# Second layers of stages 5 and 6 by block products, and a shorter conversion of the f64 weights

## The chip, the cores and the metric

One core of one Trainium2 chip. The metric is the device time of the kernel in microseconds (us). TensorE (PE) multiplies, VectorE (DVE), ScalarE (ACT) and GpSimd (POOL) do the elementwise work, SyncE (SP) issues most DMAs. PEld is the loading of a matmul's stationary operand, which runs beside the matmuls. Each engine works through its own queue in order.

## The reference

```python
def reference(q, k, v, probs, w1, w2, w_in, w_out, alpha):
    x = attn(q, k, v)                  # 2 x 8 heads, 576 tokens, head size 64, causal window of 64
    x = x.transpose(0, 2, 1, 3).reshape(1152, 512)
    p = probs / (probs.sum(-1, keepdims=True) + 1e-9)
    y = 0
    for e in range(4):                 # w1[e]: 512 x 1024, w2[e]: 1024 x 512
        y += p[:, e:e+1] * (np.maximum(x @ w1[e], 0) @ w2[e])
    h = y @ w_in                       # 512 x 2048, float64 in memory
    g = np.maximum(h, 0) + alpha * np.minimum(h, 0)
    return (g @ w_out).astype(np.float32)   # w_out: 2048 x 512, float64 in memory
```

## The kernel before

Every matmul operand is split into a high part in fp32r and a low part (the difference), and a product is three matmuls: high x low, low x high, high x high. The high part is made by ACT, the low part by DVE (`low`, L222) or POOL.

After the attention the work goes in stages 0 to 11 of 512 hidden columns each. Stages 0 to 7 are the four experts of the first layer pair (two stages each), stages 8 to 11 the second pair. In each stage from 1 on, the tokens come in two parts: the first 512 (p = 0) and the last 640 (p = 1). The first layer of a part is seven products ("A", 0 to 6) of a Strassen-Winograd scheme over halves of the inner dimension, hidden columns and tokens (`product`, L452). Their sums are built in three PSUM banks X, Z and W that go on accumulating after a partial sum has been copied or added out. An eviction (`evict`, L506) applies the ReLU or the leaky ReLU; for stages 8 and up that is ACT `r`, DVE product with alpha, ACT `hh`, POOL `hl` (`activate`, L553). The second layer of a part is one unit ("B", `l2_unit` L584) per 128 tokens: twelve matmuls of 512 columns into one bank, added by DVE into `acc` (L692, L696). Only the last stage has its second layer of the last 512 tokens in seven block products ("M", `block_product` L646), two groups of six matmuls with 256 columns each, again with banks X, Z and W.

A PSUM bank for a new tile is handed out in the order in which the eight banks fell free.

The order of the units is written out (L787 to 816). Beside each unit, after its matmuls are issued, a planner (`plan`) hangs work on it: the weight sums and splits of the next stage, the splits of this stage's second-layer weights, the sums and splits of x. Low parts of splits are put off to the next unit (`settle`). Loads of weights (`load_w`) are hung on the unit in which the second last tile before them has had its last use.

`w_in` and `w_out` come as float64 words. 32 pieces of 128 x 512 are converted to fp32 and stored to DRAM (`conv_steps`, L264), from where stages 8 to 11 load them. A piece is three steps: two ACT operations on the low and the high word; two DVE operations (clamp, shift) and the store of the piece before; a DVE operation that puts the sign in, and a load two pieces ahead. After these come, at the start of the next step, a DVE operation for the exponent and two POOL operations. How many steps run after a unit is said by `pace` (L917): stages 2 to 6 have 13 a stage, one after every second-layer unit and four in the first layers. `EARLY` = 26 pieces are done by the end of stage 7's first layer, the rest begins in stage 8's second layer of the last 640 tokens.

Of the kernel before, what the change touches and what calls it, by code (L numbers as in the profile page):

```python
# [26 lines left out]
def tile_kernel(ctx, tc, q, k, v, probs, w1, w2, w_in, w_out, alpha, out):  # L27
# [137 lines left out]
    def load_d(n):  # L165
        which, s, f = F64[n]
        o = (s - S1) * FS + f * P
        src = w_in.bitcast(U32)[:, 2 * o:2 * o + 2 * P] if which == 1 else w_out.bitcast(U32)[o:o + P, :]
        t = late["mid"].tile([P, 1024], U32, tag="wd", bufs=2, name=f"wd{n}")
# [89 lines left out]
        while converted[0] < n:  # L259
            next(late["steps"], None)  # L260

    EARLY = 13 * len(F64) // 16

    def conv_steps(first, last):  # L264
        done = []

        def store():
            if done:
                o, y = done.pop(0)
                nc.sync.dma_start(out=o, in_=y)  # L270
                converted[0] += 1

        late["ct"] = big_as("ct").rearrange("p (o m) -> p o m", o=7)
        load_d(first)
        load_d(first + 1)
        yield
        for n, (which, s, f) in list(enumerate(F64))[first:last]:
            ct = late["ct"]
            t = wd_t.pop(n)
            if which == 1:  # L280
                words = t.rearrange("p (k m w) -> p k m w", k=KD, w=2)
                top, low = words[:, :, :, 1], words[:, :, :, 0]
# [163 lines left out]
    tr = {}  # L446
# [52 lines left out]
    def h_tiles(s, p, f):  # L499
        if (s, p, f) not in h_t:  # L500
            pool = late["mid"] if p else sb
            h_t[s, p, f] = [pool.tile([P, LEN[p]], F32R, tag=f"h{w}{p}", bufs=NF, name=f"h{w}{s}_{p}_{f}")
                            for w in "hl"]
        return h_t[s, p, f]

    def evict(s, p, f, half, src, direct=False):  # L506
        c = slice(half * HALF[p], (half + 1) * HALF[p])
        hh, hl = [x[:, c] for x in h_tiles(s, p, f)]
        if s >= S1:
# [43 lines left out]
    def activate(keep, later):  # L553
        while len(heads) > keep:
            hh, hl, r, col, src, g = heads.pop(0)
            nc.vector.scalar_tensor_tensor(out=g, in0=r, scalar=col, in1=src, op0=ALU.mult, op1=ALU.add)
            tails.append((hh, hl, g))
# [151 lines left out]
    with tc.manual_schedule():  # L709
# [68 lines left out]
        def Bt(s, p):  # L778
            return [("B", s, p, t) for t in range(NTT[p])]

        def LC(c):
            return [("LC", c, f) for f in range(NF)]

# [22 lines left out]
                last_use[op] = len(order) - 1  # L806
        order += [("END",)] + LC(3) + [("X1",)] + BC(3)
        for s in range(1, S1):
            order += A(s, 0) + A(s, 1) + Bt(s, 0) + Bt(s, 1)
        order += A(S1, 0) + [("B", S1, 0, t) for t in (2, 3, 0, 1)]  # L810
        order += A(S1, 1) + [("B", S1, 1, t) for t in (3, 4, 0, 1, 2)]
        for s in range(S1 + 1, NST - 1):
            order += A(s, 0) + A(s, 1) + Bt(s, 0) + Bt(s, 1)
# [11 lines left out]
        for s in range(1, NST):  # L825
            if s == 1:
                lc, b = [[(k, NCH - 1, t) for t in range(3)] for k in ("LC", "BC")]
                for u in range(2):
                    plan(lc[u], w_sums, (1, s), s, u, nc.gpsimd)
                for u, part, unit in ((0, A11, ("X1",)), (1, A11, b[0]), (0, SA1, b[0]), (1, SA1, b[1]),  # L830
                                      (0, A22, b[2]), (1, A22, b[2])):
                    plan(unit, w_split, (1, s), s, u, part)
            else:
                b = [("B", s - 1, x, t) for x in range(2) for t in range(NTT[x])]
                if s == S1 + 1:
                    b = [("B", S1, 1, t) for t in (3, 3, 4, 4, 0, 1)]
                late_sums = s > S1 + 1
                behind = 2 * (s > S1 + 1)
                plan(b[1] if behind else ("A", s - 1, 1, 0 if s > S1 else 2), w_sums, (1, s), s, 0, nc.gpsimd)
                for n, part in ((0, A11), (0, A22), (1 + behind, SA1)):  # L840
                    plan(b[n], w_split, (1, s), s, 0, part)
                plan(b[2 + behind], w_sums, (1, s), s, 1, nc.gpsimd)
                for n, part in ((2, A11), (3, A22), (4 + behind, SA1)):
                    plan(b[n], w_split, (1, s), s, 1, part)
            units = [(0, 0), (0, 1), (1, 0), (1, 1)]
            if s in (1, S1):
                units = [(int(s == 1), i) for i in (0, 0, 1, 1)]
            for f, (p, i) in enumerate(units):
# [33 lines left out]
        for unit, splits, sums, e in ((lc[0], (0, 5), (), None), (lc[1], (0,), (), None), (lc[2], (), (1,), nc.vector),  # L882
# [11 lines left out]
        for unit, span in ((("A", 1, 0, 5), (0, EARLY)), (("A", S1, 1, 2), (EARLY, len(F64)))):  # L894
            plan(unit, lambda *a: late.update(steps=conv_steps(*a)) or next(late["steps"]), None, *span)
        plan(("B", S1 - 1, 0, 0), raw_tile, None)
        uses = {}
        for n in sorted(work):
# [17 lines left out]
            load_w(tid)  # L916
        def pace(op, s=0, p=0, i=0):  # L917
            if op == "A":
                return int(2 <= s < S1 and i < 2 or S1 < s < NST - 1 and i < 2)
            if op != "B" or s in (S1 - 1, NST - 2, NST - 1) or (s, p) == (S1, 0) or s > S1 and (p, i) == (0, 0):  # L920
                return 0
            return 1 + (s == 1 and p == 0 and i % 2)

        pend = []
        for i, unit in enumerate(order):
# [9 lines left out]
            if op == "A":  # L935
                product(unit[1], unit[2], 0, unit[3])
                product(unit[1], unit[2], 1, unit[3])
                if unit[3] == 6:
                    low_parts(0)
                    activate(0, 0 if unit[1] == S1 else 4)  # L940
            elif op == "M":
                activate(0, max(0, len(tails) - 1))
                block_product(*unit[1:])
# [17 lines left out]
                fn(*args)  # L961
            for _ in range(pace(*unit)):
                next(late["steps"], None)
            if i == at["A", S1 - 1, 1, 6]:
                convert(EARLY)
# [50 lines left out]
```

## Time and profile before

| | us |
|---|---|
| three runs, median (lowest, highest) | 612.62 (612.18, 613.17) |
| profiled execution | 612.78 |
| its span, first to last instruction | 611.0 |
| PE busy in it | 604.4 |
| DVE busy | 484.1 |
| ACT busy | 321.0 |
| POOL busy | 278.4 |

The profiled execution is one of its own; its time exceeds its span by what lies around the first and the last instruction. Busy times are sums over the whole span; which engine is late in a stage is read from the windows, the waits and the timeline.

### The profile page before, as it was taken

To read this page: it belongs to the slowest core of one execution; us is meant where nothing else is said; L and a number is where in the kernel's file an instruction comes from. 1 tells how busy PE (TensorE), PEld (TensorE's weight loads), DVE (VectorE), ACT (ScalarE), POOL (GpSimd) and SP (SyncE) were. 2 spreads that over 40 slices of the span, in tenths; PEclk is the share of its full clock that TensorE was granted. 3 is DMA by queue.
4 is the path that set the end of the run, shared out by engine and by line. 5 is a ranking of instruction groups with operands and counts; after the bars stand their busy time and mean duration, and the time that the engine had idled before them with its cause. 6 is when DMAs were issued, how large, how long until landed. Compare 5 with 4: busy or idle time off the path is not lost.

```text
span 611.0 us, 11073 instructions
## 1 busy us (share of the span) xinstructions
PE 604.4 (99%) x4108; PEld 549.2 (90%) x4108; DVE 484.1 (79%) x971; ACT 321.0 (53%) x801; POOL 278.4 (46%) x285
## 2 busy tenths in 40 slices
PE   7999999999999999999999999999999999999997
PEld 6898899889889889989989989989898988988987
DVE  4788597799798798798698698657968979756785
ACT  6966356436427426426515625536777653653750
POOL 4815812075153254265152452522755586664450
PEclk9999999999999999999999999999999999999999
DMA  8924005235235225324325323012302402300012
GB/s 277 378 92 139 2 1 162 78 106 165 95 104 156 92 98 170 108 72 170 104 93 152 120 87 104 17 70 78 130 1 74 165 38 82 122 41 1 2 53 103
DMA packets 31830, 62.61 MB, mean 102 GB/s; under 512 B 2464, under 2 KB 11936, under 8 KB 30752
## 3 DMA queue, kind: packets, MB, share of 16 engines
q1 hardware_dynamic: 31056, 61.25, 29.9%
q8 instruction: 32, 0.52, 0.4%
q10 hardware_dynamic: 720, 0.66, 0.3%
q14 instruction: 22, 0.18, 0.1%
HBM read 51.14 MB, written 10.75 MB: 101 GB/s over the span
## 4 chain that ended last, share of the span: by engine, by line
PE 97%; ACT 2%; DMA 1%; DVE 0%; ACTq 0%; issue 0%
PE o L580 42%; PE X L465 23%; PE Z L465 12%; PE W L465 6%; PE h L535 4%; PE oc L568 4%; PE pv L391 1%; ACT p L358 1%; PE pt L374 1%; PE mX L667 1%; PE s L336 1%; DMA kt<-in_k_dram 1%; PE x L706 1%; PE mZ L667 0%; PE mW L667 0%; ACT ptr L380 0%
## 5 line engine op out<-in xcount | busy, mean ns | idle before, releaser
L580 PE MATMUL o<-w2h,hl 128*128 128x512 f32 x380 | 148.2, 390 | 0.0
L580 PE MATMUL o<-w2l,hh 128*128 128x512 f32 x380 | 148.2, 390 | 0.0
L580 PE MATMUL o<-w2h,hh 128*128 128x512 f32 x380 | 148.0, 389 | 0.0
L305 POOL TENSOR_TENSOR ct<-ct 128x512 f32<-128x512 f32 x32 | 44.3, 1383 | 115.5 <-DVE ct L304 53.2
L580 PEld LDWEIGHTS o<-w2h,hl 128*128 128x128 f32 x380 | 71.3, 188 | 15.7 <-POOL hl L561 0.7
L580 PEld LDWEIGHTS o<-w2h,hh 128*128 128x128 f32 x380 | 71.3, 188 | 14.4
L580 PEld LDWEIGHTS o<-w2l,hh 128*128 128x128 f32 x380 | 71.3, 188 | 14.1
L692 DVE SCALAR_TENSOR_TENSOR acc<-o,pn,acc 128x512 f32<-128x512 f32 x63 | 47.1, 747 | 38.9 <-PE o L580 38.7
L199 POOL TENSOR_TENSOR sr<-ws 128x256 f32<-128x256 f32 x44 | 41.6, 945 | 74.1 <-DVE wfl L223 61.0
L223 DVE SCALAR_TENSOR_TENSOR w2l<-ws,w2h 128x512 fp32r<-128x512 f32 x48 | 43.7, 923 | 19.0 <-ACT w2h L230 18.9
L465 PE MATMUL X<-xth,wfl 128*128 128x256 f32 (+1 forms) x264 | 56.7, 296 | 0.0
L465 PE MATMUL X<-xtl,wfh 128*128 128x256 f32 (+1 forms) x264 | 56.6, 295 | 0.0
L465 PE MATMUL X<-xth,wfh 128*128 128x256 f32 (+1 forms) x264 | 56.6, 295 | 0.0
L230 ACT ACTIVATE wfh<-sr 128x1024 fp32r<-128x1024 f32 x22 | 23.2, 1059 | 53.5 <-POOL sr L199 53.5
L306 POOL TENSOR_TENSOR ct<-ct 128x512 f32<-128x512 f32 x32 | 47.3, 1478 | 2.5
L293 ACT ACTIVATE ct<-wd 128x512 f32<-128x512 f32 x32 | 21.4, 667 | 48.3 <-DVE ct L299 48.3
L465 PEld LDWEIGHTS X<-xtl,wfh 128*128 128x128 f32 x264 | 42.7, 190 | 0.0
L465 PEld LDWEIGHTS X<-xth,wfh 128*128 128x128 f32 x264 | 42.6, 190 | 0.0
L465 PEld LDWEIGHTS X<-xth,wfl 128*128 128x128 f32 x264 | 42.6, 190 | 0.0
L465 PE MATMUL Z<-xth,wfl 128*128 128x320 f32 (+1 forms) x176 | 37.8, 296 | 0.0
L465 PE MATMUL Z<-xtl,wfh 128*128 128x320 f32 (+1 forms) x176 | 37.7, 295 | 0.0
L465 PE MATMUL Z<-xth,wfh 128*128 128x320 f32 (+1 forms) x176 | 37.7, 295 | 0.0
(212 smaller groups left out, 1430.3 us busy)
## 6 DMA issues: line engine op xcount, KB each, us to landing
ws<-in_moe_w_dram SPq DMA_DIRECT2D x15, 1024.0 KB, 6.5
wd<-in_moe_w_in_dram SPq DMA_DIRECT2D x16, 512.0 KB, 3.7
cv<-ct SPq DMA_DIRECT2D x32, 256.0 KB, 2.6
wd<-in_moe_w_out_dram SPq DMA_DIRECT2D x16, 512.0 KB, 3.5
ws<-cv SPq DMA_DIRECT2D x8, 1024.0 KB, 5.2
v<-in_v_dram SPq DMA_DIRECT2D x16, 256.0 KB, 5.7
out_dram<-acc SPq DMA_DIRECT2D x7, 256.0 KB, 2.0
q<-in_q_dram SPq DMA_DIRECT2D x4, 384.0 KB, 7.5
```

What stands on the lines that cost most here:

```text
L199: e.tensor_tensor(out=t4[:, o], in0=x, in1=y, op=op)
L223: nc.vector.scalar_tensor_tensor(out=lv, in0=src, scalar=1.0, in1=hv.bitcast(F32), op0=ALU.mult, op1=ALU.subtract)
L230: nc.scalar.activation(out=hv, in_=src, func=AF.Copy)
L293: nc.scalar.activation(out=a, in_=top.bitcast(F32), func=AF.Abs, scale=LIFT)
L305: nc.gpsimd.tensor_tensor(out=y, in0=y, in1=e, op=ALU.mult)
L306: nc.gpsimd.tensor_tensor(out=y, in0=r, in1=y, op=ALU.add)
L336: nc.tensor.matmul(sv[hp][c, 0:w].rearrange("p (n t) -> p n t", t=BLK), lhsT=qs[g % 3][r, jb, hp, :], rhs=kts[b][r, lo:i + 1, hp, :], star ...
L465: nc.tensor.matmul(ps, lhsT=w[:, d, :], rhs=x[:, d, :], start=(first and m == 0), stop=(m == 5), skip_group_check=True)
L535: nc.tensor.matmul(ps, lhsT=w[:, d * P:(d + 1) * P], rhs=x[:, d, 0:n], start=(m == 0), stop=(m == 3 * KD - 1))
L568: nc.tensor.matmul(ps, lhsT=h_c[c, f][a][:, t * P:(t + 1) * P], rhs=w_t[2, 0, f][b], start=(n == 0), stop=(n == 3 * NF - 1))
L580: nc.tensor.matmul(ps, lhsT=h_t[s, p, f][a][:, t * P:(t + 1) * P], rhs=w_t[2, s, f][b][:, cols], start=(n == 0), stop=(n == 3 * NF - 1))
L692: nc.vector.scalar_tensor_tensor(out=at, in0=ps, scalar=sc, in1=at, op0=ALU.mult, op1=ALU.add)
```

## The change

The first 512 tokens of the second layers of stages 5 and 6 (`FORMS`) are done by seven block products ("F", 0 to 6) in place of four units, in the order F0 F1 B3 F2 F3 B4 F4 F5 F6 B0 B1 B2, where B are the five units of the last 640 tokens. The sums of h and of the weights are made by POOL in place (`form_sum`) from raw copies of h (an added ACT copy in `evict`) and from the raw weights; their high parts are made by ACT, their low parts by DVE (`form_part`). The sums and splits of the next stage's first-layer weights move to F2 and later units.

The conversion drops the exponent operation and one of two POOL operations (an integer add in place of a multiply and an add), uses two tiles for the high word, and loads three pieces ahead, every third piece into the `ct` tile. It runs in three segments: pieces 0 to 24 in stages 1 to 4, 25 to 28 in the first layers of stage 7, and 29 to 31 from stage 8's unit A3 of the last 640 tokens on; none in stages 5, 6, 9 and 10.

```diff
+    FORMS = (5, 6)
...
+        if n % 3 == 2:
+            t = late["ct"][:, 5:7].rearrange("p o m -> p (o m)").bitcast(U32)
+        else:
+            t = late["mid"].tile([P, 1024], U32, tag="wd", bufs=2, name=f"wd{n}")
...
-    EARLY = 13 * len(F64) // 16
+    SEGMENTS = (0, 25, 29, len(F64))
...
-            a, r, y, e = [view(ct[:, o]) for o in (0, 1 + n % 2, 4 + n % 3, 3)]
-            au, ru, eu = [x.bitcast(U32) for x in (a, r, e)]
-            nc.scalar.activation(out=y, in_=low, func=AF.Copy, scale=2.0 ** -52)
+            a, y = [view(ct[:, o]) for o in (n % 2, 2 + n % 3)]
+            au, yu = [x.bitcast(U32) for x in (a, y)]
+            nc.scalar.activation(out=yu, in_=low, func=AF.Copy, scale=2.0 ** -29)
             nc.scalar.activation(out=a, in_=top.bitcast(F32), func=AF.Abs, scale=LIFT)
             yield
             nc.vector.tensor_scalar(out=a, in0=a, scalar1=LOW, scalar2=HIGH, op0=ALU.max, op1=ALU.min)
             nc.vector.tensor_scalar(out=au, in0=au, scalar1=3, scalar2=None, op0=ALU.logical_shift_left)
             store()
             yield
-            nc.vector.scalar_tensor_tensor(out=ru, in0=top, scalar=SIGN, in1=au,
+            nc.vector.scalar_tensor_tensor(out=au, in0=top, scalar=SIGN, in1=au,
                                            op0=ALU.bitwise_and, op1=ALU.bitwise_or)
-            if n + 2 < last:
-                load_d(n + 2)
+            if n + 3 < last:
+                load_d(n + 3)
             yield
-            nc.vector.tensor_scalar(out=eu, in0=ru, scalar1=EXPO, scalar2=None, op0=ALU.bitwise_and)
-            nc.gpsimd.tensor_tensor(out=y, in0=y, in1=e, op=ALU.mult)
-            nc.gpsimd.tensor_tensor(out=y, in0=r, in1=y, op=ALU.add)
+            nc.gpsimd.tensor_tensor(out=yu, in0=au, in1=yu, op=ALU.add)
...
+        if raw is not None:
+            nc.scalar.activation(out=raw, in_=src, func=AF.Relu)
+        if hh is not None:
+            nc.scalar.activation(out=hh, in_=src, func=AF.Relu)
+            lows.append((hl, src, hh))
...
+    def form_raw(s):
+        g = [late["wfp"].tile([P, 4, 2, P], F32, tag="sr", bufs=1, name=f"ga{s}").rearrange(
+            "p (n f) k m -> p n f (k m)", n=2), wide(s, "gb")]
+        quarter[s] = {(1, 0): g[0][:, 0], (0, 1): g[0][:, 1], (1, 1): g[1][:, 0], (0, 0): g[1][:, 1]}
...
+    def form_sum(s, key, n):
...
+        nc.gpsimd.tensor_tensor(out=raw[i], in0=raw[j], in1=raw[k], op=op)
...
+    def form_part(s, key, n):
...
+        if any(r):
+            pending.append(lambda: [low(as_r(cut(lo, f)), raw[:, f], as_r(cut(hi, f))) for f in range(2)])
+        else:
+            pending.append(lambda: low(as_r(lo), raw, as_r(hi)))
...
+    def form_product(s, n):
+        left, right, bank, i, j = BLOCKS[n]
+        for x in range(2):
+            first = (s, bank, x) not in banks
...
+            if s < S1:
+                nc.vector.scalar_tensor_tensor(out=o, in0=ps, scalar=pn[:, t, s // SPE:s // SPE + 1], in1=o,
+                                               op0=ALU.mult, op1=ALU.add)
...
+        def layer(s):
+            if s not in FORMS:
+                return Bt(s, 0) + Bt(s, 1)
+            f, b = [("F", s, n) for n in range(7)], [("B", s, 1, t) for t in (3, 4, 0, 1, 2)]
+            return f[0:2] + b[0:1] + f[2:4] + b[1:2] + f[4:7] + b[2:]
...
+                if s - 1 in FORMS:
+                    behind = 2
+                    b = layer(s - 1)
+                    b = [b[n] for n in (2, 3, 4, 5, 6, 8, 9)]
...
+                for n, unit in ((0, ("A", s, 0, 5)), (1, ("A", s, 0, 5)), (2, ("A", s, 0, 6)), (3, ("A", s, 1, 2))):
+                    plan(unit, form_sum, (2, s), s, "b", n)
+                for n in range(4):
+                    plan(("A", s, 1, int(s >= S1)), form_sum, None, s, "a", n)
+                for key, n, unit in (("b", 1, ("A", s, 1, 1)), ("b", 0, ("A", s, 1, 2)), ("a", 1, ("A", s, 1, 6)),
+                                     ("a", 0, ("F", s, 0)), ("b", 2, ("F", s, 1)), ("a", 2, ("B", s, 1, 3)),
+                                     ("a", 3, ("F", s, 2)), ("b", 3, ("F", s, 3))):
...
         def pace(op, s=0, p=0, i=0):
             if op == "A":
-                return int(2 <= s < S1 and i < 2 or S1 < s < NST - 1 and i < 2)
-            if op != "B" or s in (S1 - 1, NST - 2, NST - 1) or (s, p) == (S1, 0) or s > S1 and (p, i) == (0, 0):
+                if s < S1 - 1:
+                    return int(2 <= s < FORMS[0] and (p, i) in ((0, 6), (1, 0), (1, 2)))
+                return int(s == S1 - 1 or s == S1 and p == 1 and i > 2)
+            if op != "B" or s in FORMS or s > S1 or s == S1 - 1:
                 return 0
-            return 1 + (s == 1 and p == 0 and i % 2)
+            if s == S1:
+                return 2 * p
+            return 2 if s > 1 or i % 2 == 0 else 1
...
+            elif op == "F":
+                activate(0, max(0, len(tails) - 2))
+                form_product(*unit[1:])
```

## Rows read from the trace of the kernel before

**Rows 1.** The page, part 4: the chain that ended last, by engine.

```profile
PE 97%; ACT 2%; DMA 1%; DVE 0%; ACTq 0%; issue 0%
```

**Rows 2.** Windows: stretch, its us, PE, PEld, DVE, ACT, POOL busy, clock, DMA.

```profile
228.86:251.25 22.39, 22.39 (x170) 22.39 (x169) 20.06 (x38) 13.44 (x34) 9.27 (x8) 1.00 0.51 165
251.25:275.76 24.51, 24.51 (x111) 20.27 (x110) 19.71 (x27) 7.91 (x14) 11.44 (x9) 1.00 0.23 74
275.76:322.66 46.90, 46.90 (x278) 42.66 (x278) 39.50 (x65) 21.49 (x46) 19.89 (x18) 1.00 0.35 119
```

**Rows 3.** Waits of PEld: waiter, releaser, us in total, times, longest.

```profile
PEld o L580 <- POOL hl L561: 0.7, 2, 0.4
```

**Rows 4.** The chain in order of time: start, us, what.

```profile
204.35 24.51 PE o L580 x108
...
597.72 1.43 PE mX L667 x12
...
606.35 1.43 PE mX L667 x12
```

**Rows 5.** Groups by form, conversion: operation and count | busy us, mean ns | idle before.

```profile
L292 ACT ACTIVATE ct<-wd 128x512 f32<-128x512 uint32 x32 | 21.1, 661 | 13.5 <-DMA wd<-in_moe_w_in_dram 10.3 <-DMA wd<-in_moe_w_out_dram 3.2
...
L295 DVE TENSOR_SCALAR ct<-ct 128x512 f32<-128x512 f32 x32 | 27.7, 865 | 0.0
L296 DVE TENSOR_SCALAR ct<-ct 128x512 uint32<-128x512 uint32 x32 | 26.6, 832 | 1.1
...
L299 DVE SCALAR_TENSOR_TENSOR ct<-wd,ct 128x512 uint32<-128x512 uint32 x32 | 29.3, 915 | 0.4
...
L304 DVE TENSOR_SCALAR ct<-ct 128x512 uint32<-128x512 uint32 x32 | 15.6, 487 | 0.2
...
L305 POOL TENSOR_TENSOR ct<-ct 128x512 f32<-128x512 f32 x32 | 44.3, 1383 | 115.5 <-DVE ct L304 53.2 <-ACT wfh L230 22.7 <-issue 11.8
...
L306 POOL TENSOR_TENSOR ct<-ct 128x512 f32<-128x512 f32 x32 | 47.3, 1478 | 2.5
```

**Rows 6.** Groups by form: evictions, low parts of weights, weight sums.

```profile
L692 DVE SCALAR_TENSOR_TENSOR acc<-o,pn,acc 128x512 f32<-128x512 f32 x63 | 47.1, 747 | 38.9 <-PE o L580 38.7
L223 DVE SCALAR_TENSOR_TENSOR w2l<-ws,w2h 128x512 fp32r<-128x512 f32 x48 | 43.7, 923 | 19.0 <-ACT w2h L230 18.9
...
L679 DVE TENSOR_TENSOR acc<-mX,acc 128x256 f32<-128x256 f32 x6 | 2.6, 425 | 1.2 <-PE mX L667 1.2
...
L199 POOL TENSOR_TENSOR sr<-ws 128x256 f32<-128x256 f32 x44 | 41.6, 945 | 74.1 <-DVE wfl L223 61.0 <-DMA ws<-in_moe_w_dram 13.2
```

**Rows 7.** Timeline, stages 3 and 7: start, us, engine, operation [idle before].

```profile
204.27 1.08 DVE L524 SCALAR_TENSOR_TENSOR hl<-X,hh 128x320 fp32r<-128x320 f32 x2
...
207.80 0.42 DVE L295 TENSOR_SCALAR ct<-ct 128x512 f32<-128x512 f32 x1
...
371.05 1.40 DVE L296 TENSOR_SCALAR ct<-ct 128x512 uint32<-128x512 uint32 x1
...
374.68 0.68 DVE L223 SCALAR_TENSOR_TENSOR w2l<-ws,w2h 128x512 fp32r<-128x512 f32 x1
...
370.82 1.35 POOL L305 TENSOR_TENSOR ct<-ct 128x512 f32<-128x512 f32 x1 [3.46 <-ACT s L472]
```

**Rows 8.** The page, part 6: DMA issues, KB each, median us to landing.

```profile
ws<-in_moe_w_dram SPq DMA_DIRECT2D x15, 1024.0 KB, 6.5
```

**Rows 9.** Windows, stage 8, end of the first layer of the last 640 tokens.

```profile
449.08:454.86 5.78, 5.78 (x39) 5.57 (x38) 5.78 (x12) 4.88 (x11) 4.65 (x5) 1.00 0.00 0
```

**Rows 10.** Timeline of DVE, ACT and POOL in the same stretch.

```profile
451.52 0.48 DVE L476 TENSOR_TENSOR u<-Z,u 128x320 f32<-128x320 f32 x1
...
453.01 1.85 DVE L556 SCALAR_TENSOR_TENSOR u<-r,alph,u 128x320 f32<-128x320 f32 x2
...
450.14 0.47 ACT L512 ACTIVATE r<-z 128x320 f32<-128x320 f32 x1
...
454.46 1.97 POOL L561 TENSOR_TENSOR hl<-u,hh 128x320 fp32r<-128x320 f32 x2
```

More of the change, by code (lines that the diff above doesn't have):

```diff
@@ L273, in conv_steps @@
         late["ct"] = big_as("ct").rearrange("p (o m) -> p o m", o=7)
-        load_d(first)
-        load_d(first + 1)
+        for n in range(first, min(first + 3, last)):
+            load_d(n)
         yield
@@ L508, in evict @@
         hh, hl = [x[:, c] for x in h_tiles(s, p, f)]
+        raw = None
+        if p == 0 and s in FORMS:
+            raw = quarter[s][half, f // 2][:, f % 2, :]
+            if (half, f // 2) == (1, 0):
+                hh = hl = None
         if s >= S1:
@@ new lines, in evict, with wide @@
+        if hh is not None:
+            nc.scalar.activation(out=hh, in_=src, func=AF.Relu)
+            lows.append((hl, src, hh))
+    lows = []
+    quarter, form = {}, {}
+    def wide(s, name):
+        return late["mid"].tile([P, 1024], F32, tag="wd", bufs=2, name=f"{name}{s}").rearrange(
+            "p (n f m) -> p n f m", n=2, f=2)
+    def form_raw(s):
+        g = [late["wfp"].tile([P, 4, 2, P], F32, tag="sr", bufs=1, name=f"ga{s}").rearrange(
+            "p (n f) k m -> p n f (k m)", n=2), wide(s, "gb")]
+        quarter[s] = {(1, 0): g[0][:, 0], (0, 1): g[0][:, 1], (1, 1): g[1][:, 0], (0, 0): g[1][:, 1]}
+        w = ws_t[2, s]
+        b = {(i, j): w[:, 2 * i:2 * i + 2, HC * j:HC * (j + 1)] for i in range(2) for j in range(2)}
+        form[s, "a", "raw"] = [quarter[s][x] for x in ((1, 1), (0, 0), (1, 0), (0, 1))]
+        form[s, "b", "raw"] = [b[x] for x in ((0, 0), (1, 1), (0, 1), (1, 0))]
@@ new lines, in form_room @@
+    def form_room(s):
+        big = big_as(f"sf{s}").rearrange("p (n f m) -> p n f m", n=7, f=2)
+        big = [big[:, n] for n in range(7)]
+        pair = wide(s, "fa")
+        bits = [late["mid"].tile([P, HALF[1]], F32, tag="tr", bufs=5, name=f"fb{s}_{f}")[:, 0:HC] for f in range(5)]
+        bits.append(late["wfp"].tile([P, HC], F32, tag="ex", bufs=1, name=f"fc{s}"))
+        hh, hl = [[h_tiles(s, 0, f)[n][:, HALF[0]:] for f in range(2)] for n in range(2)]
+        form[s, "a", 0] = [hh, pair[:, 0], hl, bits[0:2]]
+        form[s, "a", 1] = big[4:7] + [bits[2:4]]
+        form[s, "b", 0] = big[0:4]
+        form[s, "b", 1] = [bits[4:6], pair[:, 1], None, None]
@@ new lines, in form_part, with high @@
+    def form_part(s, key, n):
+        hi, lo, raw = [form[s, key, w][n] for w in (0, 1, "raw")]
+        r = [isinstance(x, list) for x in (hi, lo)]
+        def high(o, x):
+            nc.scalar.activation(out=as_r(o), in_=x, func=AF.Copy)
+        if r[0]:
+            for f in range(2):
+                high(hi[f], raw[:, f])
+        else:
+            high(hi, raw)
+        if any(r):
+            pending.append(lambda: [low(as_r(cut(lo, f)), raw[:, f], as_r(cut(hi, f))) for f in range(2)])
+        else:
+            pending.append(lambda: low(as_r(lo), raw, as_r(hi)))
@@ new lines, in cut, with as_r @@
+    def cut(x, f):
+        return x[f] if isinstance(x, list) else x[:, f]
+    def as_r(x):
+        return x if x.dtype == F32R else x.bitcast(F32R)
+    def form_product(s, n):
+        left, right, bank, i, j = BLOCKS[n]
+        for x in range(2):
+            first = (s, bank, x) not in banks
+            if first:
+                banks[s, bank, x] = psum(f"f{bank}{s}_{x}")[:, 0:HC]
+            ps = banks[s, bank, x]
+            m = 0
+            for f in range(2):
+                for a, b in ((0, 1), (0, 0), (1, 0)):
+                    if left[0] == "a":
+                        o = HC * left[1] + P * x
+                        lhs = h_t[s, 0, 2 * left[2] + f][a][:, o:o + P]
+                    else:
+                        lhs = as_r(cut(form[s, "a", a][left[1]], f))[:, P * x:P * (x + 1)]
+                    if right[0] == "b":
+                        rhs = w_t[2, s, 2 * right[1] + f][b][:, HC * right[2]:HC * (right[2] + 1)]
+                    else:
+                        rhs = as_r(cut(form[s, "b", b][right[1]], f))
+                    nc.tensor.matmul(ps, lhsT=lhs, rhs=rhs, start=(first and m == 0), stop=(m == 5),
+                                     skip_group_check=True)
+                    m += 1
+            t = 2 * i + x
+            o = acc[0][:, t, HC * j:HC * (j + 1)]
+            if s < S1:
+                nc.vector.scalar_tensor_tensor(out=o, in0=ps, scalar=pn[:, t, s // SPE:s // SPE + 1], in1=o,
+                                               op0=ALU.mult, op1=ALU.add)
+            else:
+                nc.vector.tensor_tensor(out=o, in0=ps, in1=o, op=ALU.add)
@@ L556, in activate @@
             nc.vector.scalar_tensor_tensor(out=g, in0=r, scalar=col, in1=src, op0=ALU.mult, op1=ALU.add)
-            tails.append((hh, hl, g))
+            if hh is not None:
+                tails.append((hh, hl, g))
         while len(tails) > later:
@@ L808, in tile_kernel @@
         for s in range(1, S1):
-            order += A(s, 0) + A(s, 1) + Bt(s, 0) + Bt(s, 1)
+            order += A(s, 0) + A(s, 1) + layer(s)
         order += A(S1, 0) + [("B", S1, 0, t) for t in (2, 3, 0, 1)]
@@ L812, in tile_kernel @@
         for s in range(S1 + 1, NST - 1):
-            order += A(s, 0) + A(s, 1) + Bt(s, 0) + Bt(s, 1)
+            order += A(s, 0) + A(s, 1) + layer(s)
         s = NST - 1
@@ L893, in tile_kernel @@
                     plan(unit, x_sum, None, 1, xr[1], f, o, w, e)
-        for unit, span in ((("A", 1, 0, 5), (0, EARLY)), (("A", S1, 1, 2), (EARLY, len(F64)))):
-            plan(unit, lambda *a: late.update(steps=conv_steps(*a)) or next(late["steps"]), None, *span)
+        for unit, n in ((("A", 1, 0, 5), 0), (("A", S1 - 1, 0, 0), 1), (("A", S1, 1, 2), 2)):
+            plan(unit, lambda *a: late.update(steps=conv_steps(*a)) or next(late["steps"]), None, *SEGMENTS[n:n + 2])
         plan(("B", S1 - 1, 0, 0), raw_tile, None)
@@ L963, in tile_kernel @@
                 next(late["steps"], None)
-            if i == at["A", S1 - 1, 1, 6]:
-                convert(EARLY)
+            for n, last in enumerate((("B", FORMS[0] - 1, 1, NTT[1] - 1), ("A", S1 - 1, 1, 6), ("B", S1, 1, 2))):
+                if unit == last:
+                    convert(SEGMENTS[n + 1])
             for tid in loads.get(i, ()):
```

26 lines of the change are left out of this document (19 added, 7 removed).

## The prediction

> **What bounds the kernel now.** I read the chain of waits first. It is TensorE for 97% [rows 1]. The windows then show that inside a stage it has no hole: PE is busy for all of the 22.39, 24.51 and 46.90 us of the pieces shown, at a clock of 1.00, with VectorE (DVE) at 80 to 90% behind it [rows 2]. So a gain can come only from fewer or shorter matmuls. Anything done on ACT, DVE or POOL costs nothing until it reaches a matmul late. The list of waits names where that is already so in the stages: in stage 8 two weight loads of second-layer units waited 0.7 us together for POOL's low parts `hl` [rows 3]. That place decides my forecast.
>
> **The gain.** A second layer of stages 1 to 7 is 9 units of 12 matmuls with 512 columns in 24.51 us, 2.72 a unit; the four units of the first 512 tokens take 10.89 [rows 4]. The seven products of the last stage have the shape of the new ones (12 matmuls of 256 columns). The first begins at 597.72, the last ends at 606.35 + 1.43 = 607.78: 10.06 [rows 4]. So 0.83 us a stage, 1.66 for two; the clock is at its upper level of 2.4 GHz in both. A matmul of 256 columns costs 120 ns against 227 for 512, not half.
>
> A rule of the Trainium skill would give more: "TensorE: Matmul & The Clock Gate", section "Back-to-back issue gap", puts the isolated gap at columns over 2.4 GHz plus 2.5 ns, from which I estimate 48 x 216 - 84 x 109 ns = 1.2 us a stage. The rows hold the two shapes themselves and decide; the page also says that the weight load has its share in the spacing, which fits 120 ns.
>
> **What stages 5 and 6 get beside it.** 13 conversion steps a stage go away (4.33 pieces: 13.4 us of DVE at 865 + 832 + 915 + 487 ns, 12.4 us of POOL at 1383 + 1478) [rows 5]. In come, a stage: eight sums of 512 columns on POOL (bounded by the conversion's two POOL rows: 11 to 12 us); eight splits, their low parts on DVE (923 ns mean, 0.68 when undisturbed) [rows 6, 7]; 14 evictions of 256 columns (425 ns) for four of 512 (747 ns) [rows 6]; eight raw copies on ACT. DVE comes out lighter by some 4 us, POOL level, and ACT, at 21 of 47 us, has room [rows 2]. On average that is covered; the tight place is the queue order inside the products. Banks X and Z take up accumulation again after DVE has added them out, so F6 can't start before DVE has evicted F4. From F0 to F6 PE needs 6 x 1.44 + 2 x 2.72 = 14.1 us. Ahead of that eviction in DVE's queue stand a rest of the first layer (the low parts of X, done 1.0 us after PE began the second layer [rows 4, 7]), eight evictions (3.4), two of 512 (1.5), six low parts of the forms and three of the next stage's weights (8.5 in units of 512 columns: 5.8 at 0.68 each, 7.8 at 0.923), and its own first half (0.4): 12.1 to 14.1 us, plus about 0.4 in which DVE waits for the second unit. So 0 to 0.4 late at these rows, up to 1.2 if POOL's weight sums, which start in this stretch, hold the last two low parts. I take 0.3 a stage, 0.6 in all, and keep 0 to 2.4.
>
> The new wait there: POOL's weight sums for the next stage, moved into F2, use the tile in which half of the raw `h` lies, so they start only behind the low part of form 3 (about 11 us after F0's start). Behind them POOL holds only the second set of sums. ACT's split of them waits, and DVE's low part of that split stands ahead of the evictions of F5 and F6. Four sums take 3.8 us [rows 6], so DVE is through these near 18. The next units take banks that fell free earlier, and the next stage wants the weights at 25: cost 0, and a stall only if it slips by 7 us. The next second-layer weights are loaded behind the last form's low part (12.6); 6.5 us to land [rows 8] is 19, wanted at 25: 0.
>
> **Stages 2 to 4.** They do 21 steps (7 pieces) instead of 13, 18 of them in the second half. That half has 19.71 us of DVE in 24.51 with three pieces [rows 2]; without their 9.3 it is 10.4. Six new pieces (865 + 832 + 915 ns, the exponent's 487 gone) make 26.1 with it at mean durations, 19.5 at the undisturbed 0.42 + 0.42 + 0.68 [rows 5, 7] (shift and sign step taken like the clamp and the low part that the rows show undisturbed). I take the middle, 23: it fits. What hides a lag is eight PSUM banks and a first half where DVE has 20.06 of 22.39 with four steps and gets three. Cost 0, up to 1 us a stage if it piles up. Stage 7 does four pieces within its first layer; its second layer is lighter for DVE, and I take 0, up to 0.5. POOL's integer add has no row; bounds are the float ones (1.4 us) and double, which would equal the two that it replaces: off the path in either case. Conversions on SP gain a third load in flight, nothing on the path. Stages 9 and 10 lose theirs: PE had no hole there, so nothing.
>
> **Stage 8, the loss.** Three pieces remain, and their steps now follow units 3 to 6 of the first layer for the last 640 tokens; before, the first came in the second layer. There the chain is DVE sum, ACT `r`, DVE product, ACT `hh`, POOL `hl`, and TensorE reads the result at once: DVE is at work for all of 449.08 to 454.86, with ACT at 4.88 and POOL at 4.65 of these 5.78 us [rows 9]; ACT's `r` of z starts at 450.14 with no idle time ahead of it, and the `hl` of u end at 454.46 + 1.97 = 456.43 [rows 10], while the weight loads already wait [rows 3]. Step one puts two ACT operations (661 ns each [rows 5], the second taken like the first, 1.2 together with their overlap) ahead of that `r`; POOL gets its next `hh` later by as much. Step two puts clamp and shift on DVE ahead of the sum of u at 451.52 [rows 10]: 0.84 undisturbed, up to 1.40 each beside POOL, as the shift that began 0.2 us into a POOL operation and ended 0.3 after it [rows 7]. Step three puts the sign step ahead of the second product of u: 0.68 to 0.92 [rows 5, 7]. POOL's own add comes behind the last `hl` and hurts nobody. Sum 2.7 to 4.9, less what overlaps (while ACT is late, DVE's wait and POOL's gap absorb some): I take 2.6 and keep 1.0 to 4.5. Slack is zero, since PE waits for these `hl` today.
>
> **Sum.** -1.66 + 0.6 + 2.6 = +1.5 on the profiled execution, 612.78 with a span of 611.0 and 1.8 around it: 614.3. That execution lies 0.16 above the median of the runs shown (612.62), so 614.2.
>
> **Rivals.** (B) Faster: stage 8's steps cost nothing, because the chain before `hl` of u has give that the rows don't show (gaps of ACT and POOL in that window, 0.9 and 1.1 us [rows 9], that take up the new work), and F6 isn't late: 612.62 - 1.66 = 611.0, up to 611.4. For it: those gaps, and that the waits of today are short. Against: DVE has no gap there. It decides if the steps add under 0.4. (C) Half covered: 1.0 to 1.8 in stage 8 and little in F6, 612.0 to 613.2: no change that can be measured (0.2%, 1.2 us, is what runs of this kernel can tell). For it: the undisturbed durations. (D) Contention in full: each of the three DVE steps in stage 8 lasts as long as the POOL operation beside it (about 1 us each [rows 10]), 4.2 there, and F6 is 0.8 late in both stages: 612.62 - 1.66 + 4.2 + 1.6 = 616.8, and 615.4 with F6 at 0.1. For it: the 1.40 us row [rows 7]. Against: the mean rows of 0.83 to 0.92 hold undisturbed ones too.
>
> The Trainium skill bears on (D): "GPSIMD Engine Reference", section "Specifications", says that POOL shares its SBUF interfaces with VectorE, with contention for VectorE instructions in a two-port mode or with two SBUF inputs, which would be all three steps. The row of 1.40 against 0.42 agrees, and by that rule alone the time would be (D)'s 615.4 to 616.8.
>
> **Chances.** Forecast (613.2 to 615.2 in itself) 0.43; B 0.22; C 0.18; D 0.17. Below 611.4: B, 0.21. Within 0.2% (611.4 to 613.85): C and the lower third of the forecast's span, 0.32. Above: 0.47. The range of 611.1 to 615.9 leaves out half of B's best case and half of D.
>
> **What would show it.** Right: idle time of the weight loads at the first second-layer unit of stage 8 grows from 0.7 to some 3 us with POOL `hl` or ACT `hh` as releaser; a second layer of stages 5 and 6 takes 23.7 us plus a small hole before F6 released by DVE; stages 2 to 4 stay 46.90. Wrong: stage 8 without a hole, or a hole elsewhere, as in a first layer of stage 7 (DVE's sum of z late for bank X) or where a half of stages 2 to 4 grows.

## The result and the profile after

The changed kernel takes 616.33 us (median of 4 runs, 615.86 to 617.23) against 612.71 us (4 runs on the same chip, 612.18 to 613.17): a ratio of 1.0061, 95% interval [1.0044, 1.0079]. It is slower by 0.6%, more than I forecast; 616.33 lies outside my range. The profiled execution of after took 616.02 us with a span of 614.1.

Busy times of the page, part 1, after: the clock stays at 1.00, TensorE does 0.6 us more, DVE and POOL much less.

```profile
PE 605.0 (99%) x4180; PEld 551.3 (90%) x4180; DVE 466.3 (76%) x979; ACT 331.2 (54%) x835; POOL 250.3 (41%) x269
```

DVE had 484.1 us and POOL 278.4 before; only ACT has more, 331.2 for 321.0. So the work of DVE and POOL really became lighter, and that bought nothing. The waits of the weight loads (PEld) between 87 and 600.5 us say where the time went; before, this list had one line, 0.7 us [rows 3]. Columns: waiter, releaser, us in total, times, longest.

```profile
PEld o L684 <- POOL hl L665: 2.2, 3, 0.8
PEld o L684 <- ACT hh L664: 2.1, 2, 1.5
PEld fX L613 <- DVE acc L619: 1.6, 2, 0.8
PEld X L467 <- DVE z L478: 0.6, 3, 0.2
```

Three places, then: stage 8 (lines 1 and 2), the seventh block product (line 3, once in each of stages 5 and 6), and the first layers' bank X (line 4, three times). The windows give their sizes. Stretches of after: first and second layer of stage 5 (stage 6 has the same two lengths, 22.64 and 24.58), first layer of stage 7, and stage 8's second layer of the last 640 tokens. Columns as in [rows 2].

```profile
274.50:297.14 22.64, 22.64 (x170) 22.45 (x168) 19.48 (x34) 14.75 (x38) 12.59 (x10) 1.00 0.21 70
297.14:321.72 24.58, 23.99 (x147) 21.36 (x145) 19.07 (x37) 8.14 (x18) 6.74 (x8) 1.00 0.24 79
...
368.94:391.65 22.71, 22.71 (x169) 22.40 (x168) 19.57 (x39) 15.11 (x36) 8.33 (x7) 1.00 0.30 105
...
453.54:470.93 17.39, 15.02 (x62) 10.95 (x61) 14.73 (x20) 10.95 (x23) 11.03 (x12) 1.00 0.04 15
```

Windows of before, stage 8's second layer and stage 9's first, which the groups ahead of the prediction do not hold:

```profile
453.68:467.75 14.07, 14.07 (x63) 11.11 (x62) 10.83 (x16) 10.51 (x20) 8.53 (x10) 1.00 0.10 31
467.75:490.14 22.39, 22.39 (x170) 22.39 (x168) 20.41 (x35) 15.69 (x41) 12.81 (x12) 1.00 0.46 158
```

Against 22.39 and 24.51 [rows 2] and 14.07: the first layers of stages 5, 6 and 7 are longer by 0.25, 0.25 and 0.32 us, the second layers of stages 5 and 6 by 0.07 each instead of shorter, stage 8's by 3.32. All other stages keep their lengths. That is 4.28 us, and it is what the timeline gives from the first matmul of stage 2 to the first block product of the last stage: 466.94 (133.80 to 600.74) against 462.66 (134.90 to 597.56). The profiled executions differ by only 3.2 us because stage 2 began 1.1 us earlier in that of after; in the eight executions profiled here it began anywhere from 133.3 to 135.0, so I compare stages and not spans. The medians differ by 3.62 us, 0.66 less than the stages; the start of stage 2 scatters by more than that, and what makes up the 0.66 is not shown.

Conversion, groups by form of after (operation and count | busy us, mean ns | idle before); [rows 5] hold before.

```profile
L308 POOL TENSOR_TENSOR ct<-ct 128x512 uint32<-128x512 uint32 x32 | 45.6, 1431 | 101.2 <-DVE ct L303 59.4 <-ACT s L474 13.4 <-PE W L467 10.4
L299 DVE TENSOR_SCALAR ct<-ct 128x512 f32<-128x512 f32 x32 | 23.9, 747 | 4.1 <-ACT ct L297 4.1
...
L300 DVE TENSOR_SCALAR ct<-ct 128x512 uint32<-128x512 uint32 x32 | 16.7, 523 | 1.1
```

The integer addition takes 1431 ns, like one of the two float operations it replaces. Clamp and shift are unchanged instructions, and their means fell from 865 and 832 ns.

**Stage 8.** Timeline of after, ACT, DVE and POOL: start, us, engine, operation [idle before].

```profile
449.89 0.67 ACT L296 ACTIVATE ct<-ct 128x512 uint32<-128x512 uint32 x1
...
451.01 0.47 ACT L519 ACTIVATE r<-z 128x320 f32<-128x320 f32 x1
...
451.98 1.10 DVE L299 TENSOR_SCALAR ct<-ct 128x512 f32<-128x512 f32 x1
453.12 0.98 DVE L300 TENSOR_SCALAR ct<-ct 128x512 uint32<-128x512 uint32 x1
454.02 0.48 DVE L478 TENSOR_TENSOR u<-Z,u 128x320 f32<-128x320 f32 x1
...
455.74 1.36 DVE L303 SCALAR_TENSOR_TENSOR ct<-ct 128x512 uint32<-128x512 uint32 x1
457.02 1.15 DVE L659 SCALAR_TENSOR_TENSOR u<-r,alph,u 128x320 f32<-128x320 f32 x1
...
452.76 1.05 POOL L665 TENSOR_TENSOR hl<-z,hh 128x320 fp32r<-128x320 f32 x1
...
455.54 1.01 POOL L665 TENSOR_TENSOR hl<-z,hh 128x320 fp32r<-128x320 f32 x1 [1.73 <-ACT hh L664]
```

Read it against [rows 10], with 0.14 us taken off before's times, since the kernel reached this place that much earlier here. The `r` of z is 1.0 us late behind ACT's step (two operations like the one shown); clamp and shift hold the sum of u until 454.02, 2.6 late by now; the sign step holds the second product of u until 457.02. The steps put in 1.0 + 2.04 + 1.28 = 4.3 us; the stage grew by 3.32, so 1.0 was absorbed. All three DVE steps ran beside a POOL operation.

**The seventh product.** Timeline of after, stage 5, DVE, POOL and PE.

```profile
308.57 0.75 DVE L796 SCALAR_TENSOR_TENSOR acc<-o,pn,acc 128x512 f32<-128x512 f32 x1 [0.41 <-PE o L684]
309.24 1.16 DVE L227 SCALAR_TENSOR_TENSOR fd<-ws,sf 128x512 fp32r<-128x512 f32 x1
310.32 1.22 DVE L227 SCALAR_TENSOR_TENSOR wfl<-ws,wfh 128x512 fp32r<-128x512 f32 x1
311.47 0.86 DVE L619 SCALAR_TENSOR_TENSOR acc<-fX,pn,acc 128x256 f32<-128x256 f32 x2
...
309.81 1.19 POOL L203 TENSOR_TENSOR sr<-ws 128x256 f32<-128x256 f32 x1
...
311.99 0.38 PE L613 MATMUL fX<-fd,hh 128*128 128x256 f32 x1 [0.59 <-DVE acc L619]
```

The eviction of F4 (the two `acc<-fX`) stands behind two low parts of 1.16 and 1.22 us beside POOL's four weight sums, of which one is shown; undisturbed, such a low part takes 0.68 [rows 7].

**Bank X in the first layers.** Timeline of after: stage 7 (DVE, PEld), then stage 5 (DVE, POOL, PEld).

```profile
388.45 0.41 DVE L299 TENSOR_SCALAR ct<-ct 128x512 f32<-128x512 f32 x1
388.90 0.43 DVE L300 TENSOR_SCALAR ct<-ct 128x512 uint32<-128x512 uint32 x1
389.24 0.48 DVE L478 TENSOR_TENSOR z<-X,z 128x320 f32<-128x320 f32 x1
...
389.78 0.30 PEld L467 LDWEIGHTS X<-xth,wfl 128*128 128x128 f32 x2 [0.25 <-DVE z L478]
...
281.00 1.28 DVE L627 SCALAR_TENSOR_TENSOR hl<-s,hh 128x256 fp32r<-128x256 f32 x1
...
279.33 2.67 POOL L569 TENSOR_TENSOR ws<-ws 128x512 f32<-128x512 f32 x2 [1.40 <-DVE w2l L227]
...
283.27 0.30 PEld L467 LDWEIGHTS X<-xth,wfl 128*128 128x128 f32 x2 [0.19 <-DVE z L478]
```

In stage 7 a conversion step stands ahead of the sum of z that empties bank X. In stage 5 no conversion is left, but the new sums of the block forms run on POOL, and a low part of 256 columns beside them takes 1.28 us; the sum of z is late behind it.

### The profile page after: what moved, and what is told of

Read it like the earlier page. It is cut to its first block, busy times and chain, and to the rows that moved or that the text cites. A ratio compares the mean times of both kernels' runs of the same rounds, so it can differ in the third digit from the quotient of the medians.

```text
span 614.1 us, 11271 instructions
## 1 busy us (share of the span) xinstructions
PE 605.0 (99%) x4180; PEld 551.3 (90%) x4180; DVE 466.3 (76%) x979; ACT 331.2 (54%) x835; POOL 250.3 (41%) x269
## 5 line engine op out<-in xcount | busy, mean ns | idle before, releaser
L684 PE MATMUL o<-w2l,hh 128*128 128x512 f32 x348 | 136.1, 391 | 1.5 <-ACT hh L664 1.5
L684 PE MATMUL o<-w2h,hl 128*128 128x512 f32 x348 | 135.9, 391 | 0.9 <-POOL hl L665 0.9
L684 PE MATMUL o<-w2h,hh 128*128 128x512 f32 x348 | 135.5, 389 | 0.0
L308 POOL TENSOR_TENSOR ct<-ct 128x512 uint32<-128x512 uint32 x32 | 45.6, 1431 | 101.2 <-DVE ct L303 59.4
L684 PEld LDWEIGHTS o<-w2h,hl 128*128 128x128 f32 x348 | 65.3, 188 | 16.1 <-POOL hl L665 2.2
L684 PEld LDWEIGHTS o<-w2l,hh 128*128 128x128 f32 x348 | 65.3, 188 | 14.9 <-ACT hh L664 2.1
L796 DVE SCALAR_TENSOR_TENSOR acc<-o,pn,acc 128x512 f32<-128x512 f32 x55 | 41.1, 747 | 31.1 <-PE o L684 30.9
L227 DVE SCALAR_TENSOR_TENSOR w2l<-ws,w2h 128x512 fp32r<-128x512 f32 x48 | 37.5, 798 | 32.2 <-ACT w2h L234 32.1
L665 POOL TENSOR_TENSOR hl<-s,hh 128x256 fp32r<-128x256 f32 (+1 forms) x14 | 11.4, 831 | 64.2 <-ACT hh L664 52.4
L800 DVE TENSOR_TENSOR acc<-o,acc 128x512 f32<-128x512 f32 x23 | 15.9, 690 | 25.8 <-PE o L684 25.8
```

The costliest lines, as they stand in the source:

```text
L227: nc.vector.scalar_tensor_tensor(out=lv, in0=src, scalar=1.0, in1=hv.bitcast(F32), op0=ALU.mult, op1=ALU.subtract)
L308: nc.gpsimd.tensor_tensor(out=yu, in0=au, in1=yu, op=ALU.add)
L684: nc.tensor.matmul(ps, lhsT=h_t[s, p, f][a][:, t * P:(t + 1) * P], rhs=w_t[2, s, f][b][:, cols], start=(n == 0), stop=(n == 3 * NF - 1))
L796: nc.vector.scalar_tensor_tensor(out=at, in0=ps, scalar=sc, in1=at, op0=ALU.mult, op1=ALU.add)
L800: nc.vector.tensor_tensor(out=at, in0=ps, in1=at, op=ALU.add)
```

## The experiments

Theory after the result: four local terms, each a piece of DVE or ACT work put ahead of one result that a matmul waits for. Rivals: the new form of the conversion or of the products costs something spread over the kernel; or each repair only hands the wait on. Times of before on the same chip: 612.32 us (29 runs) for the first four kernels, 611.83 (17 runs) for the last two.

**Stage 8's steps only in its second layer.**

```diff
-                return int(s == S1 - 1 or s == S1 and p == 1 and i > 2)
+                return int(s == S1 - 1)
```

> The changed kernel, but stage 8's conversion steps run only after its second-layer units. Theory (the steps in the first layer delay the chain DVE sum, ACT r, DVE product, ACT hh, POOL hl that TensorE waits for): the first second-layer unit of the last 640 tokens loses its holes, stage 8 gets 3.3 us shorter, 613.0 us (612.5 to 613.5). Rival (the three pieces have no room in stage 8 at all, and the hole only moves to the first layer of stage 9): 615 to 616.3.

Measured: 613.72 us (12 runs), ratio 1.0022 [1.0012, 1.0032]. Windows, stage 8's second layer and stage 9's first; then the waits of PEld from 453 to 600 us:

```profile
453.62:467.69 14.07, 14.07 (x63) 11.11 (x62) 9.35 (x14) 8.96 (x19) 8.48 (x10) 1.00 0.00 0
467.69:491.12 23.43, 22.73 (x169) 22.50 (x168) 19.85 (x35) 17.03 (x43) 11.50 (x11) 1.00 0.33 124
```

```profile
PEld Z L467 <- DVE wfl L227: 0.9, 1, 0.9
PEld o L684 <- POOL hl L665: 0.7, 2, 0.4
```

Stage 8 is back at 14.07, with the 0.7 us wait of before. But the time was 0.7 above the centre of what I expected, outside its range and short of the rival's: three whole pieces now run behind the first layer, the low parts of stage 9's first weights come late on DVE, and 1.04 us come back there.

**Only the first step, ACT's, in stage 8's first layer.**

```diff
-                return int(s == S1 - 1 or s == S1 and p == 1 and i > 2)
+                return int(s == S1 - 1 or s == S1 and p == 1 and i == 3)
```

> The changed kernel, but of stage 8's steps only the first (two ACT operations) stays in the first layer; DVE's clamp, shift and sign step come in the second layer. Theory (delay is the sum of ACT's 1.1 us and DVE's three operations beside POOL): 1.0 us more than e1, 614.0 us (613.6 to 614.5). Rival (DVE's operations alone count, ACT has gaps enough): as e1, 613.0. Rival (ACT's delay starts it all): 615.5 to 616.3.

Measured: 613.68 us (10 runs), ratio 1.0026 [1.0015, 1.0037]. Windows, stage 8's second layer and stage 9's first:

```profile
454.68:469.35 14.67, 14.43 (x63) 10.96 (x62) 12.86 (x17) 11.29 (x22) 10.86 (x12) 1.00 0.05 18
469.35:491.74 22.39, 22.39 (x170) 22.39 (x169) 17.61 (x34) 15.63 (x41) 9.74 (x10) 1.00 0.35 119
```

ACT's step costs 0.60 us; by subtraction, the DVE steps make the other 2.7 where they stand in after. Moved behind the first layer they cost nothing, and stage 9's first layer is back at 22.39. The time alone is that of the first experiment and would fit the first rival; the windows tell them apart, since 0.60 stands in stage 8 here and 1.04 stood in stage 9 there.

**Block products off, the conversion's new schedule kept.** The planner still empties stages 5 and 6 of conversion steps.

```diff
-    FORMS = (5, 6)
+    FORMS, DONE = (5, 6), ()
...
-            if s not in FORMS:
+            if s not in DONE:
```

> The changed kernel without the block products: stages 5 and 6 have their four units as before, the conversion's schedule stays as changed. Theory (stage 8's 3.3 and stage 7's 0.3 us are the conversion's; the block products as placed cost 0.6 net in two stages): 615.7 us (615.2 to 616.2), stages 2 to 6 at 46.90 us. Rival (the holes in stages 5 and 6 are due to the conversion crowded into stages 2 to 4, and the block products gain): stages 5 and 6 above 46.90, 616.5 or more.

Measured: 615.39 us (4 runs), ratio 1.0048 [1.003, 1.0066]. Windows, stage 5's first layer and stage 8's second:

```profile
274.86:297.25 22.39, 22.39 (x170) 22.39 (x168) 17.08 (x35) 12.90 (x31) 4.66 (x6) 1.00 0.37 118
...
453.11:470.51 17.40, 15.05 (x62) 10.95 (x61) 14.72 (x20) 10.95 (x23) 11.04 (x12) 1.00 0.04 16
```

Stage 5's first layer is as before to the hundredth (its second takes 24.51 again), and stage 8 has its 3.33. So the longer first layer of stage 5 belongs to the block forms and the loss of stage 8 to the schedule; stage 7 loses 0.22, and with 0.05 gained elsewhere the stages lose 3.50 us in all. With the products on, each of stages 5 and 6 is 0.32 us longer than here (0.25 and 0.07): with all that feeds them the products cost time instead of saving it.

**The kernel before with conversion steps in stage 8's first layer.**

```diff
-                return int(2 <= s < S1 and i < 2 or S1 < s < NST - 1 and i < 2)
+                return int(2 <= s < S1 and i < 2 or s == S1 and p == 1 and i > 2 or S1 < s < NST - 1 and i < 2)
```

> The kernel before, with one thing added: a step of its own old conversion schedule after each of the last four units of stage 8's second first-layer group. Theory (the 3.3 us of the change in stage 8 come from conversion work that stands on ScalarE and VectorE among the evictions of those 256 tokens, whatever the conversion's own form): the 640-token second layer of stage 8 grows from 14.07 us by 2 to 3.5 us, the later stages stay at 22.39 and 24.51 us, and the time is 614.4 to 615.9 us against 612.4. Rival (the cost belongs to the new form of the conversion, above all its integer addition on GpSimd, or to loads three pieces ahead): the second layer stays within 0.5 us of 14.07 and the time within 0.5 us of the kernel before.

Measured: 618.12 us (4 runs), ratio 1.0107 [1.0093, 1.0122]. Windows, stage 8's second layer and stage 9's first; the waits of PEld from 453 to 500 us, without the two lines of stage 8, which are those of after, and a last one of 0.3:

```profile
453.30:470.72 17.42, 15.06 (x62) 10.95 (x61) 14.61 (x19) 9.34 (x20) 12.51 (x13) 1.00 0.25 76
470.72:496.43 25.71, 23.43 (x169) 22.55 (x168) 22.45 (x36) 18.23 (x46) 15.88 (x14) 1.00 0.48 154
```

```profile
PEld X L465 <- ACT u L472: 1.6, 2, 1.0
PEld X L465 <- DVE z L476: 1.3, 1, 1.3
```

Stage 8 grows by 3.35 us with the old form of the conversion and the old loads, as the theory asked; the rival (new form, integer add, loads) falls. The time overshot my expectation by 2.2 us: stage 9's first layer, which holds conversion steps in before too, grew by 3.32 as well: DVE has 22.45 us of work there for 20.41, and bank X waits. I had not foreseen that second place. The four steps put forward also change which step of a piece falls on which unit of stage 9; what of that makes the 3.32 there was not tried.

**Four repairs, one kind in stage 5 and another in stage 6.** Stage 8 as in the first experiment; no step at one unit of stage 7; stage 5: the weight splits up to two units earlier, and an ordinary unit between F5 and F6; stage 6: the first form sum ahead of the others and two form parts three units later, and one low part of the next weights moved from F3 to F5.

```diff
-            return f[0:2] + b[0:1] + f[2:4] + b[1:2] + f[4:7] + b[2:]
+            if s == FORMS[0]:
+                return f[0:2] + b[0:1] + f[2:4] + b[1:2] + f[4:6] + b[2:3] + f[6:7] + b[3:]
...
-                    b = [b[n] for n in (2, 3, 4, 5, 6, 8, 9)]
+                    b = [b[n] for n in ((2, 3, 4, 5, 6, 8, 8) if s - 1 == FORMS[0] else (2, 3, 7, 5, 6, 8, 9))]
...
+                if s != FORMS[0]:
+                    plan(("A", s, 0, 5), form_sum, None, s, "a", 0)
...
+                d = 3 * (s != FORMS[0])
-                for key, n, unit in (("b", 1, ("A", s, 1, 1)), ("b", 0, ("A", s, 1, 2)), ("a", 1, ("A", s, 1, 6)),
+                for key, n, unit in (("b", 1, ("A", s, 1, 1 + d)), ("b", 0, ("A", s, 1, 2 + d)), ("a", 1, ("A", s, 1, 6)),
```

> As e1, and three more places eased, by two means each so that the stages show which reason holds. Stage 5: unit B0 between F5 and F6; second-layer weights split two units earlier. Stage 6: order as changed, but the low part of the second weight half put off from the unit after F3 to the one after F5; POOL's sums of the weights held back behind the first sum of h. Stage 7: no conversion step after the unit before the sums of z. Theory (DVE's queue ahead of the eviction of F4, and ahead of the sum of z, is what PE waits for): both F6 holes of 0.85 us go, the 0.2 to 0.3 us holes at bank X in stages 5, 6, 7 go, stages 5 and 6 take 46.1 us each: 611.1 us (610.7 to 611.8), faster than before by 1.6. Rival (DVE is short of time over the whole stage, so that a moved operation is late elsewhere): holes of the same size at other units, 612.5 to 613.5. Rival for F6 alone (POOL's sums beside DVE make the delay, not the order of DVE's queue): stage 6 keeps 0.5 us or more, stage 5 none.

Measured: 611.92 us (12 runs, 611.18 to 616.71), ratio 0.9999 [0.9982, 1.0017]. Windows, the layers of stages 5 and 6:

```profile
273.97:296.74 22.77, 22.64 (x170) 22.44 (x168) 18.42 (x35) 14.94 (x39) 13.44 (x10) 1.00 0.21 70
296.74:320.50 23.76, 23.76 (x146) 21.32 (x145) 18.78 (x36) 7.73 (x17) 6.75 (x8) 1.00 0.20 67
320.50:342.89 22.39, 22.39 (x169) 22.39 (x168) 13.73 (x26) 13.92 (x36) 10.77 (x8) 1.00 0.06 25
342.89:366.63 23.74, 23.74 (x146) 21.33 (x145) 20.50 (x42) 9.10 (x20) 6.63 (x8) 1.00 0.35 111
```

Both repairs of the seventh product work (23.76 and 23.74 for 24.58). Stage 6 loses its hole with POOL's sums still beside the products, so the rival for F6 alone falls. Of those for bank X the earlier splits do not (22.77), the moved form work does (22.39). The time lies 0.1 above the range that I expected and below the rival's: the gain is eaten by stage 9's 1.05, as in the first experiment, and stage 5's 0.38.

**The repairs that worked, in both stages.** The form work of both stages is moved as it was for stage 6 above. The last three pieces now go in single steps in stage 8's second layer (last group) and in stage 9, where before had its tail.

```diff
-                    b = [b[n] for n in (2, 3, 4, 5, 6, 8, 9)]
+                    b = [b[n] for n in (2, 3, 7, 5, 6, 8, 9)]
...
-                return int(s == S1 - 1 or s == S1 and p == 1 and i > 2)
+                return int(s == S1 - 1 and (p, i) != (1, 3) or s == S1 + 1 and i < 2)
...
-            if s == S1:
-                return 2 * p
+            if s >= S1:
+                return int((s, p) != (S1, 0) and (s == S1 or (p, i) != (0, 0)))
```

> The changed kernel with every repair that a stage's length bore out, in both stages 5 and 6: the form sum of the left side ahead of the others and two of the right-hand parts three units later (no late sum of z for bank X), the low part of the next stage's weights put off so that the eviction of the fifth block product is not behind it, no conversion step at the one unit of stage 7, and the last three conversion pieces in single steps in stage 8's second group of token tiles and in stage 9 instead of stage 8 alone. Theory (the four terms add up and each is removed): first layers 22.39 us in stages 5 to 9, second layers of stages 5 and 6 23.75 us instead of 24.51, stage 8's 14.07, so 1.5 us below the kernel before: 610.9 us, ratio 0.9975. Rival (each repair only hands the wait on to a later unit, as the 1.04 us that came back in stage 9 when stage 8's steps were put off): some first layer after stage 5 is again longer than 22.6 us and the time is 611.9 us or above.

Measured: 610.35 us (12 runs), ratio 0.9978 [0.9963, 0.9993], expected 0.9975. Windows, stage 5's two layers, stage 8's second and stage 9's first:

```profile
275.18:297.57 22.39, 22.39 (x169) 22.39 (x168) 16.64 (x29) 13.93 (x36) 12.61 (x10) 1.00 0.22 71
297.57:321.31 23.74, 23.74 (x146) 21.33 (x145) 20.53 (x42) 9.10 (x20) 6.65 (x8) 1.00 0.18 61
...
451.74:465.85 14.11, 14.11 (x63) 11.11 (x61) 10.95 (x14) 10.51 (x20) 9.41 (x10) 1.00 0.03 12
465.85:488.24 22.39, 22.39 (x170) 22.39 (x168) 18.37 (x36) 16.60 (x43) 8.64 (x9) 1.00 0.34 111
```

PE is busy in all of each, and the only PEld wait left from stage 2 to stage 11 is the 0.7 us of before. Stage 7's first layer is 22.44, with one conversion step fewer. The four terms were separable, and without them the change gains what its products save. This kernel beats both.

## Why the prediction was wrong

The direction held, and stage 8 was the main loss, but the sum came out as +4.28 on the stages where I had +1.5. Of the 2.7 between them the seventh product makes 1.1, the first layers of stages 5, 6 and 7 make 0.8, stage 8 makes 0.7 and the gain 0.1. The mechanism that I named for stage 8 and for the seventh product is the one that came; their sizes failed, and bank X of the first layers was put at 0.

- **Gain, -1.66.** Right: 24.51 - 23.74 = 0.77 a stage once the hole is gone, 1.54 in all. The 1.2 us a stage that I estimated from the isolated gap of the Trainium skill ("TensorE: Matmul & The Clock Gate", "Back-to-back issue gap") is not reached; the rows of the last stage were the better price.
- **Seventh product, +0.6.** Mis-sized: 24.58 - 23.74 = 0.84 a stage, 1.68. I had written down the case that came, POOL's sums holding the last two low parts, at up to 1.2, and then took 0.3, a value between free and held. But a wait for one named pair of operations is met or not: the sums start when form 3's low part frees their tile, which by my own working was just then, so the pair met them each time, alike in both stages.
- **Stages 5 and 6, first layer, 0, and stage 7, 0.** Wrong: 0.25, 0.25 and 0.32. For stages 5 and 6 I compared DVE's busy total with its room and looked for a deadline only inside the products; the bank of a first layer has one as well. I had named bank X in stage 7 only as a sign of error.
- **Stage 8, +2.6.** The largest miss in one place: 3.32. The steps themselves came to 4.3, inside the 2.7 to 4.9 I wrote but above its middle of 3.8; 1.0 of it was absorbed, near the 1.2 that I took off from that middle. So 0.5 of the miss lies in the durations and 0.2 in the overlap. The sizes were contended ones: 1.10, 0.98 and 1.36 against 0.41 and 0.43 in stage 7 (shown above) and, for the sign step, the 0.68 of an undisturbed low part [rows 7]; the sign step alone lay beyond the 0.68 to 0.92 that I gave it, by holding the queue for 1.28.
- **Rivals.** D, contention in full, had 615.4 to 616.8 and a chance of 0.17; the time fell inside it. Its parts were not quite those: stage 8 cost less than its 4.2, and bank X supplied the rest. B and C are refuted by stage 8's 3.32. Stages 2 to 4 stayed at 46.90 as forecast, and the integer add, the loads and the late start of the weight sums have no wait of their own in the list; the sums cost by what they did to the two low parts.

On contention: the same low part took 1.16 us beside POOL's sums in after, 0.79 beside them in the best kernel and 0.68 where POOL is idle (304.50, the same kind two units earlier). The eight traces hold many more such pairs. From 87 to 600 us, with no POOL operation beside them, all 81 clamps took 0.41 to 0.43 us, all 143 sign steps 0.67 to 0.70 and all 81 low parts `wfl<-ws,wfh` of 128 x 512 took 0.68 to 0.69. With one beside them for over half of their length, some stayed as short, and the longest of the three kinds took 1.55, 1.78 and 1.78. The 464 evictions that read PSUM (`acc<-o,pn,acc`) took 0.73 to 0.75 either way. The Trainium skill, "GPSIMD Engine Reference", "Specifications", lists as contenders DVE instructions with two SBUF inputs or in a two-port mode; the low parts agree, and an eviction with one of its two tensors in PSUM would not be one, which agrees too.

In the first layers of stages 5 and 6 the best kernel tries it: DVE's order up to the sum of z is that of after, POOL's form sum comes later, the low part takes 0.42 us for 1.28 (281.69 below), and the wait for bank X is gone. In stage 8 and before the seventh product no run took POOL's work away with DVE's order kept. There the durations allow an estimate: undisturbed, the three DVE steps of stage 8 would have held the queue for 1.5 us and not 3.3, and the two low parts ahead of F4's eviction would have been 1.0 us shorter, more than the hole of 0.84.

Timeline of DVE in the best kernel, stage 5:

```profile
281.69 0.42 DVE L627 SCALAR_TENSOR_TENSOR hl<-s,hh 128x256 fp32r<-128x256 f32 x1
...
304.50 0.68 DVE L227 SCALAR_TENSOR_TENSOR fd<-ws,sf 128x512 fp32r<-128x512 f32 x1
...
309.67 0.79 DVE L227 SCALAR_TENSOR_TENSOR fd<-ws,sf 128x512 fp32r<-128x512 f32 x1
310.38 0.86 DVE L619 SCALAR_TENSOR_TENSOR acc<-fX,pn,acc 128x256 f32<-128x256 f32 x2
```

The eviction of F4 (310.38) follows the low part at once here: the weights' low part that stood between them, 1.22 us in after, is gone from that place, and the hole with it.

## What to carry to other kernels

Where one engine is full and others have room on average, price an edit by deadlines: list each result that the full engine takes back soon (a bank, an operand), and for each the queue ahead of it with contended durations, the first layers as well as the part that was rewritten. Filler work costs anything from nothing to most of its length, by the unit it stands behind: the first four steps of the last three conversion pieces cost 3.3 us in one place; with all the steps behind the first layer the pieces cost 1.05, and spread in single steps next to nothing. Where the engine's own row shows no gap, put the contended durations into the sum and take little off for overlap: here 4.3 us of steps became 3.3.

## What the runs showed of the hardware

- GpSimd's 32-bit integer addition of 128x512 takes 1431 ns, as its float multiplication and addition do (1383 and 1478 [rows 5]).
- The means of VectorE's unchanged clamp and shift fell from 865 and 832 to 747 and 523 ns with a change that halved GpSimd's part of a conversion and also moved the steps. Alone they take 0.41 to 0.43 us each time; in the eight traces every one that took longer had a GpSimd operation beside it. With one input in PSUM, VectorE's evictions of 128x512 took 0.73 to 0.75 us, whatever GpSimd did.
